# Reordering max and score tiles inside the stretches of a fused attention and MLP kernel

## The chip, the cores and the metric

The kernel runs on one core of a Trainium2 chip. A core has engines that run side by side, each with its own in-order queue: TensorE (PE, matmuls; its weight loads are listed apart as PEld), VectorE (DVE), ScalarE (ACT), GpSimd (POOL) and SyncE (SP, which issues the DMA transfers). They meet at semaphores. The metric is the device time of one execution in microseconds (us); lower is better.

## The reference

For x of shape 2048 x 640 the kernel computes a gated mix of two branches:

```
g = sigmoid(sum(x * gate_w))
q = x @ wq  (32 heads of 20);  k = x @ wk;  v = x @ wv   (one k and one v for all heads)
a = concat_heads(softmax(q k^T / sqrt(20)) v) @ wo
h = layernorm(x)                      # per token
u = gelu(h^T @ w1 + b1)               # 640 x 1728, over the token axis
b = (u @ w2 + b2)^T                   # back to 2048 x 640
out = g * a + (1 - g) * b
```

The gelu is the tanh form. Everything is float32; the products are made of a high and a low part of each operand (three matmuls: high by high, high by low, low by high).

## The kernel before

**Units.** Attention is cut into 32 units n (4 blocks of 512 queries by 8 groups of 4 heads), and each unit into 16 key blocks of 128. A *score tile* (written s, line 702) is one matmul of 62 rows by 512 columns into a PSUM bank; ACT turns it into probabilities with an exponential (line 711, tile p). The softmax needs each row's maximum first, and it is computed by *max tiles* (written m, line 490): the same product the other way round, reduced over the free axis by DVE (line 496, tile mp). A max tile of a later unit is made while an earlier unit's scores are. Per half of the array there are 1024 max tiles and 1024 score tiles. The probabilities of two key blocks times V are one "V group" (`pv_group`, line 737), 16 narrow matmul records in the trace, which the page's rows show as x16. Its sum is copied out by ACT (`part`, line 749, or `acc`, line 746) and added up by POOL (line 750). At the end of a unit DVE transposes, takes a reciprocal and transposes back (lines 763, 769, 777).

**Lanes and stretches.** s and m have at most 62 rows, and the MLP's matmuls (g) are cut to 64 rows, so two of them run at once in the two halves of the array. A *stretch* k is a list of g matmuls in one half (the side lane) with s and m matmuls in the other (the own lane); the halves swap in the next stretch. Then comes a V group, which takes the whole array. There are 84 stretches of the first MLP product (g at line 993, 24 g each; the first of them has no V group), 128 of the second (line 805, 20 or 21 g), 32 of the output projection of finished rows (line 938, 15 g), and after them a tail of 26 key blocks without max tiles. Ahead of them all stand the projections of x, the layer norm, the splitting of the weights, and a lead of 46 max tiles per half beside the first seven column blocks of the first product.

**What sets the order.** The order of each engine's queue is written out when the program is built; a small model of clocks (`clock`, `lanes`, `issue`; 0.232 us for an s or m, 0.147 for a g) merges the two lanes, and `bank_take` picks the PSUM bank of seven that the model frees first. The table `PATTERN` (line 1060) gives for each number of g matmuls the order of s and m in the own lane, and what the side lane has before and after its g matmuls (F). `main` trims or fills this list: the scores must be four tiles ahead of what the next V group eats, and the max tiles must be as many as `share` (line 1068) says. In the first product `share` compares the sum that the table plans with what is left; while it is over, it takes one m from the half that is more over, in stretches with k%4 = 1 alone. From the second product on it spreads what is left in proportion.

**The gelu chain.** A first-product tile ends every four stretches (k%4 = 3). `gelu` (line 534) has ACT add the bias (line 539) and puts the rest into `chain`: square (ACT, 543), the cube (`cube_p`, POOL, 560 and 561), `tanh` (ACT, 551), the product (`prod_p`, POOL, 564 and 565) and the split into high and low part (`high_p`, POOL, 582 and 583). `settle` takes one entry of the chain twice per stretch: once in the middle of the stretch's list, and once at its end, before the V group. The square comes at the end of its own stretch, the cube in the middle of the next, then an empty entry, and the tanh in the middle of the stretch with k%4 = 1.

Two halves that add into one bank must not overlap (`other_tile`, line 718): the first s or m after the last g waits for it on ACT or DVE, and the first g of the next stretch waits for that.

Of the kernel before, what the change touches and what calls it, by code (L numbers as in the profile page):

```python
# [40 lines left out]
def mix_kernel(ctx: ExitStack, tc: tile.TileContext, A_x, A_wq, A_wk, A_wv, A_wo,  # L41
# [5 lines left out]
    def f32(ap):  # L47
        return ap.bitcast(F32)
# [418 lines left out]
    def busy(engine, us):  # L467
        clock[engine] = max(clock[engine], clock["now"]) + us
# [63 lines left out]
    chain, ahead = [], []  # L532

    def gelu(d, fc, accs):
        both = fin.tile([P, D], F32, name="yo")
        xg, t1 = both[:, :HD2], both[:, HD2:]
        hi, lo = u_hi[d][:, fc, :], u_lo[d][:, fc, :]
        busy("act", 0.43)
        nc.scalar.activation(xg, accs[0][:, :HD2], AF.Identity, bias=bias[:, NS + fc:NS + fc + 1])

        def square():
            busy("act", 0.38)
            nc.scalar.activation(t1, xg, AF.Square)

        def add():
            nc.vector.tensor_add(xg, xg, accs[1][:, :HD2])  # L546
            square()

        def tanh():
            busy("act", 0.37)  # L550
            nc.scalar.activation(t1, t1, AF.Tanh, scale=GC * 0.044715)

        def high():
            nc.scalar.activation(hi, t1, AF.Copy)

        def low():
            nc.gpsimd.tensor_sub(lo, t1, f32(hi))

        def cube_p():
            nc.gpsimd.tensor_scalar(t1, t1, 1.0, 1.0 / 0.044715, op0=ALU.mult, op1=ALU.add)  # L560
            nc.gpsimd.tensor_mul(t1, t1, xg)

        def prod_p():
            nc.gpsimd.tensor_scalar(t1, t1, 1.0, 1.0, op0=ALU.mult, op1=ALU.add)
            nc.gpsimd.tensor_mul(t1, t1, xg)

        def plus(c):
            nc.scalar.activation(t1, t1, AF.Copy, bias=c)

        def mul():  # L570
            nc.gpsimd.tensor_mul(t1, t1, xg)

        def cubed():
            add()
            plus(1.0 / 0.044715)

        def tanh_plus():
            tanh()
            plus(1.0)

        def high_p():
            nc.gpsimd.tensor_copy(hi, t1)
            nc.gpsimd.tensor_sub(lo, t1, f32(hi))

        if len(accs) == 2:
            ends, ahead[:] = list(ahead), [high, low]
            if fc == PRO - 1:
                add()
                chain.extend((*ends, cube_p, None, tanh, prod_p, high_p))
            else:  # L590
                chain.extend((*ends, *[None] * (2 - len(ends)), cubed, None, None, mul, *[None] * 4, tanh_plus,
                              None, mul, None, None, None))
        else:
            chain.extend((square, cube_p, None, tanh, prod_p, high_p))

    def pop_chain():
        f = chain.pop(0) if chain else None
# [3 lines left out]
    with tc.tile_pool(name="psl", bufs=4, space=PSUM) as psl, \  # L601
# [9 lines left out]
        for fc in range(PRO):  # L611
            pu = [psb.tile([P, NB], F32, name=f"pu{r}") for r in range(2)]
            for hf in range(4):
                w1_upto(4 * fc + hf + 4)
                for f in [q_parts_due.pop(0) for _ in range(min(len(q_parts_due), 1 + fc // 5))] if fc else []:
                    f()
                wh, wl = w1t.pop(4 * fc + hf)
                for c in range(HS):
                    st = hf * HS + c
                    for k, (w, h) in enumerate(((wh, h_hi[0]), (wh, h_lo[0]), (wl, h_hi[0]))):  # L620
                        for r in range(2):
                            rows = slice(64 * r, 64 * r + 64)
                            nc.tensor.matmul(pu[r][:, :HD2], w[rows, c, :], h[rows, st, :],  # L623
                                             start=(st == 0 and k == 0), stop=(st == NS - 1 and k == 2))
                    done = [max(0, min(x, final) - skip) * LEAD // (final - skip) for x in (at, at + 1)]
                    if done[1] > done[0]:
                        lead()
                    at += 1
                    pop_chain()
                if fc == 1 and hf == 0:  # L630
                    new_q(0)
                if fc == PRO - 2 and hf == 2:
                    assert not q_parts_due
                    one_by_one[0] = False
                    fetch_max(0)
            gelu(0, fc, pu)
            if fc == PRO - 3:
                store_max(0)
# [340 lines left out]
    def b1_jobs(d, fc):  # L979
        hold = {}  # L980
        base = 4 * (d * FC + fc)

        def load():
            pass

        def mm(st, k, half):
            if not hold.get("n"):
                hold["p"], hold["n"] = ps_g.tile([P, NB], F32, name="g"), 0
            wh, wl = w1t[base + st // HS]
            w, h = ((wh, h_hi), (wh, h_lo), (wl, h_hi))[k]  # L990
            hold["n"] += 1
            r = slice(64 * half, 64 * half + 64)
            other_tile(half, nc.tensor.matmul(hold["p"][:, :HD2], w[r, st % HS, :], h[d][r, st, :],  # L993
                                              start=(hold["n"] == 1), stop=(hold["n"] == 6 * NS)))

        def done():
            gelu(d, fc, [hold["p"]])

        return load, [([[lambda h=h, st=st, k=k: mm(st, k, h) for h in range(2)]
                        for st in range(NS) for k in range(3)], done)]  # L1000
# [48 lines left out]
    def settle(wide=False):  # L1049
        for _ in range(2 if spare[0] else 1):  # L1050
            if later and (wide or spare[0] or not later[0][0]):
# [5 lines left out]
    sent, back_in = {0}, {0}  # L1057

    AHEAD, DRAIN, ENTER, FIRST = 4, 0.19, 0.138, 0.1
    PATTERN = {24: ("smssmsmmssmssmmm", "Fm"), 20: ("smsmssmmsmmssm", "mFs"), 21: ("smsmsmmssmmsmsm", "Fs"),  # L1060
               15: ("smsssmmmssms", "mFs"), 0: ("mmmmmmmmmmssss", "Fsmm")}

    def pattern(k):
        return PATTERN[len(ph[k][0]) if visits[k] else 0]

# [236 lines left out]
```

## Time and profile before

| what | value |
|---|---|
| median of 3 runs | 1632.41 us (1632.35 to 1633.01) |
| the profiled execution's own time | 1631.96 us |
| span of its trace | 1630.2 us |
| granted TensorE clock | 1.00 |
| busy: PE, DVE, ACT, POOL | 100%, 86%, 80%, 53% of the span |
| stages: lead and before, first product, second, projection, tail | to 170.7, to 665.7, to 1384.4, to 1546.5, to 1630.2 us |

The first stage of this table takes in the first two stretches of the first product. A row of the profile names the line, the engine, the operation, the output and inputs, the shapes and the count. The seven banks go from one use to the next, so a tile made by line 702 or 490 may carry the name ms, s or o of the bank; the line tells what it is. Rows of PE are modelled at their ends. A bracket at the end of a timeline row is the engine's idle time before it and what is taken to have ended it.

### The profile page before, as it was taken

The numbers are of one execution on the slowest core, as the hardware profiler recorded it, in microseconds if no ns is written. First come the engines' busy times: TensorE is split into PE (matmuls) and PEld (weight loads), VectorE is DVE, ScalarE is ACT, GpSimd is POOL, SyncE is SP. The second block draws the span as 40 slices with busy tenths as digits, with TensorE's granted clock in tenths as the row PEclk, the third lists the DMA queues.
The fourth block names the chain that finished last, engine by engine and source line by source line (L and its number), as shares of the span: only waits on it lengthen the run. The fifth ranks groups of instructions, "written<-read, shape, count | busy, mean of one in ns | idle before, by whom it ended". The sixth has DMA issues, their size and how long they took to land.

```text
span 1630.2 us, 39380 instructions
## 1 busy us (share of the span) xinstructions
PE 1622.6 (100%) x14877; PEld 1127.8 (69%) x14877; DVE 1400.5 (86%) x2404; ACT 1297.2 (80%) x2567; POOL 858.5 (53%) x974
## 2 busy tenths in 40 slices
PE   9999999999999999999999999999999999999998
PEld 7899766766676667666666666666666666666666
DVE  6689999999999999999999999899999999777723
ACT  4445778787887878888888888888888888999975
POOL 6568666767686767544544344354444432433400
PEclk9999999999999999999999999999999999999999
DMA  7655222322233223222212222222222112335421
GB/s 213 210 164 146 71 73 68 74 70 76 70 81 80 63 63 83 57 65 73 65 51 59 58 60 49 73 65 73 65 65 65 54 44 58 95 101 184 133 74 41
DMA packets 173603, 135.88 MB, mean 83 GB/s; under 512 B 32793, under 2 KB 139446, under 8 KB 173414
## 3 DMA queue, kind: packets, MB, share of 16 engines
q1 hardware_dynamic: 173126, 133.04, 29.6%
q8 instruction: 117, 1.92, 0.5%
q14 instruction: 72, 0.59, 0.1%
q10 hardware_dynamic: 288, 0.33, 0.1%
HBM read 100.27 MB, written 31.65 MB: 81 GB/s over the span
## 4 chain that ended last, share of the span: by engine, by line
PE 99%; ACT 0%; DVE 0%; issue 0%; DVEq 0%; ACTq 0%
PE ms L737 14%; PE g L805 11%; PE s L737 11%; PE s L702 9%; PE g L993 9%; PE ms L702 8%; PE ms L490 7%; PE s L490 7%; PE o L737 5%; PE pp L298 4%; PE pu L623 3%; PE o L702 3%; PE o L490 2%; PE g L938 2%; PE ml L490 1%; PE s L893 1%
## 5 line engine op out<-in xcount | busy, mean ns | idle before, releaser
L496 DVE TENSOR_REDUCE mp<-ms 128x1 f32<-128x512 f32 x859 | 566.1, 683 | 69.7 <-PE ms L490 61.9
L496 DVE TENSOR_REDUCE mp<-s 128x1 f32<-128x512 f32 x810 | 535.9, 682 | 44.1 <-PE s L490 37.9
L711 ACT ACTIVATE p<-s 128x512 f32<-128x512 f32 x906 | 534.2, 624 | 37.8 <-PE s L737 13.1
L711 ACT ACTIVATE p<-ms 128x512 f32<-128x512 f32 x847 | 498.3, 621 | 36.7 <-PE s L737 11.4
L750 POOL TENSOR_TENSOR acc<-acc,part 128x512 f32<-128x512 f32 x212 | 274.4, 1294 | 392.9 <-ACT part L749 373.9
L702 PE MATMUL s<-qst,kst 62*128 62x512 f32 x906 | 353.8, 413 | 0.0
L702 PE MATMUL ms<-qst,kst 62*128 62x512 f32 x847 | 335.5, 413 | 0.4 <-ACT p L711 0.4
L490 PE MATMUL ms<-kst,qmx 60*128 60x512 f32 x859 | 332.6, 410 | 0.3 <-ACT p L711 0.3
L490 PE MATMUL s<-kst,qmx 60*128 60x512 f32 x810 | 316.4, 409 | 0.6 <-DVE yo L546 0.5
L993 PE MATMUL g<-slot,wh 64*128 64x320 f32 x1344 | 306.8, 313 | 0.0
L993 PEld LDWEIGHTS g<-slot,wh 64*128 64x128 f32 x1344 | 221.5, 184 | 68.7 <-DVE mp L496 35.2
L129 POOL TENSOR_TENSOR wl<-wr,wh 128x512 fp32r<-128x512 f32 (+1 forms) x176 | 217.7, 1237 | 29.4 <-ACT wh L126 9.7
L737 PE MATMUL ms<-p,v_sb 128*32 128x512 f32 x1904 | 228.9, 598 | 0.0
L496 DVE TENSOR_REDUCE mp<-o 128x1 f32<-128x512 f32 x287 | 196.0, 683 | 20.5 <-PE o L490 18.3
L993 PE MATMUL g<-slot,wl 64*128 64x320 f32 x672 | 206.4, 307 | 0.0
L702 PEld LDWEIGHTS s<-qst,kst 62*128 62x128 f32 x906 | 166.7, 185 | 55.1 <-ACT p L711 31.7
L805 PE MATMUL g<-u,wh 64*128 64x320 f32 x864 | 196.7, 310 | 0.0
L805 PE MATMUL g<-slot,wh 64*128 64x320 f32 x864 | 196.3, 309 | 0.0
L702 PEld LDWEIGHTS ms<-qst,kst 62*128 62x128 f32 x847 | 156.2, 185 | 55.3 <-ACT p L711 43.0
L737 PE MATMUL s<-p,v_sb 128*32 128x512 f32 x1536 | 184.7, 598 | 0.0
L711 ACT ACTIVATE p<-o 128x512 f32<-128x512 f32 x280 | 174.1, 622 | 11.5 <-PE ms L737 5.5
L490 PEld LDWEIGHTS ms<-kst,qmx 60*128 60x128 f32 x859 | 157.5, 185 | 9.2 <-ACT p L711 3.3
(244 smaller groups left out, 3158.0 us busy)
## 6 DMA issues: line engine op xcount, KB each, us to landing
wr<-in_B_w_dram SPq DMA_DIRECT2D x136, 256.0 KB
qmx<-q_scr SPq DMA_DIRECT2D x192, 80.0 KB
qst<-q_scr SPq DMA_DIRECT2D x192, 80.0 KB
y_scr<-yo SPq DMA_DIRECT2D x16, 320.0 KB
slot<-o_scr SPq DMA_DIRECT2D x16, 320.0 KB
o_scr<-ot SPq DMA_DIRECT2D x124, 40.0 KB
o_scr<-acc SPq DMA_DIRECT2D x124, 40.0 KB
q_scr<-qh SPq DMA_DIRECT2D x19, 256.0 KB
```

The lines of the kernel that those rows point to most:

```text
L129: nc.gpsimd.tensor_sub(wl[:, :nv], wr[:, :nv], f32(wh[:, :nv]))
L298: nc.tensor.matmul(pp, w, t, start=first and n == 0, stop=not more and n == len(steps) - 1)
L490: nc.tensor.matmul(ms, qmax[n][64 * b:64 * b + 60, pr, qt * P:(qt + 1) * P], kst[64 * b:64 * b + 60, kq * NB:(kq + 1) * NB], start=True, s ...
L496: r = nc.vector.tensor_reduce(mtiles[n][:, c, kq:kq + 1], ms, axis=AX.X, op=ALU.max)
L623: nc.tensor.matmul(pu[r][:, :HD2], w[rows, c, :], h[rows, st, :], start=(st == 0 and k == 0), stop=(st == NS - 1 and k == 2))
L702: nc.tensor.matmul(s, kst[64 * b:64 * b + 62, kb * P:(kb + 1) * P], q[64 * b:64 * b + 62, pr, :], start=True, stop=True)
L711: e = nc.scalar.activation(p, s, AF.Exp, scale=SCALE)
L737: nc.tensor.matmul(o[32 * hh:32 * hh + 32, :], v_sb[:, kb + i, :], ptiles.pop((u, hh)), start=opened and i == 0, stop=(i == len(us) - 1) a ...
L750: nc.gpsimd.tensor_add(sums[0], sums[0], part)
L805: other_tile(half, nc.tensor.matmul(hold["p"][:, :HD2], w[r, i, :], u[d][r, fc, :], start=(hold["n"] == 1), stop=(hold["n"] == 6 * FC - 3)))
L938: other_tile(half, nc.tensor.matmul(hold["p"][:, :HD2], o[r, c, :], w[r, c, d * HD2:(d + 1) * HD2], start=(hold["n"] == 1), stop=(hold["n" ...
L993: other_tile(half, nc.tensor.matmul(hold["p"][:, :HD2], w[r, st % HS, :], h[d][r, st, :], start=(hold["n"] == 1), stop=(hold["n"] == 6 * NS)))
```

## The change

Three edits. In the table's entry for 24 g matmuls (first product) the own lane's order begins with an m, where it began with an s, and ends with two s, where it ended with three m; there are 8 of each as before. In the entry for 15 g (projection) the own lane has four m, where it had five, and its order alternates more. In the gelu chain one more empty entry stands ahead of the tanh, so that tanh comes at the end of the stretch with k%4 = 1, the product in the middle of the next and the split at that one's end; the last gelu of the lead keeps its chain.

```diff
@@ -591,7 +591,7 @@
         else:
-            chain.extend((square, cube_p, None, tanh, prod_p, high_p))
+            chain.extend((square, cube_p, None, None, tanh, prod_p, high_p))
@@ -1057,8 +1057,8 @@
     AHEAD, DRAIN, ENTER, FIRST = 4, 0.19, 0.138, 0.1
-    PATTERN = {24: ("smssmsmmssmssmmm", "Fm"), 20: ("smsmssmmsmmssm", "mFs"), 21: ("smsmsmmssmmsmsm", "Fs"),
-               15: ("smsssmmmssms", "mFs"), 0: ("mmmmmmmmmmssss", "Fsmm")}
+    PATTERN = {24: ("msmsmmssmsmmsmss", "Fm"), 20: ("smsmssmmsmmssm", "mFs"), 21: ("smsmsmmssmmsmsm", "Fs"),
+               15: ("smsmssmsmss", "mFs"), 0: ("mmmmmmmmmmssss", "Fsmm")}
```

## The prediction

> **What bounds the kernel now.** I read the page first: its engine lines and the chain that ended last.
>
> ```profile
> span 1630.2 us, 39380 instructions
> PE 1622.6 (100%) x14877; PEld 1127.8 (69%) x14877; DVE 1400.5 (86%) x2404; ACT 1297.2 (80%) x2567; POOL 858.5 (53%) x974
> PE 99%; ACT 0%; DVE 0%; issue 0%; DVEq 0%; ACTq 0%
> ```
>
> The chain is PE almost throughout, so the time is the sum of what PE's queue takes, and another engine counts only where it holds up a matmul. The windows view, cut where the stages begin, gives length, busy time (and instructions) of PE, PEld, DVE, ACT, POOL, then the granted clock, DMA share and GB/s:
>
> ```profile
> 170.71:665.68 494.97, 494.39 (x4661) 343.98 (x4657) 461.58 (x774) 396.43 (x801) 352.61 (x417) 1.00 0.28 72
> 665.68:1384.38 718.70, 718.35 (x6693) 480.65 (x6689) 652.99 (x1106) 612.10 (x1186) 317.62 (x348) 1.00 0.23 61
> 1384.38:1546.51 162.13, 162.13 (x1444) 103.14 (x1441) 124.67 (x211) 152.76 (x304) 66.57 (x72) 1.00 0.43 130
> ```
>
> These are the first product (82 stretches from the third on), the second product (128) and the projection (32, so 5.07 us each). DVE is 93% busy in the first; ACT is 94% busy in the third. Single stretches, cut from the first matmul after one probability-times-V group to the same point after the next:
>
> ```profile
> 292.20:298.20 6.00, 6.00 (x61) 4.20 (x57) 5.22 (x9) 4.51 (x9) 5.58 (x6) 1.00 0.54 135
> 298.20:304.26 6.06, 6.06 (x63) 4.19 (x59) 5.63 (x10) 5.40 (x11) 4.99 (x5) 1.00 0.10 27
> 406.51:412.45 5.94, 5.94 (x60) 4.18 (x57) 5.63 (x11) 4.86 (x10) 1.93 (x4) 1.00 0.39 103
> 237.13:243.62 6.49, 6.18 (x61) 4.17 (x58) 5.39 (x10) 4.98 (x10) 6.17 (x9) 1.00 0.28 74
> 285.72:292.20 6.48, 6.20 (x61) 4.17 (x57) 5.40 (x10) 4.97 (x10) 6.17 (x9) 1.00 0.30 66
> 460.52:466.76 6.24, 6.24 (x62) 4.15 (x58) 6.18 (x11) 4.62 (x9) 5.16 (x7) 1.00 0.01 1
> 622.88:629.16 6.28, 6.28 (x62) 4.36 (x58) 5.81 (x11) 4.86 (x10) 1.47 (x2) 1.00 0.37 90
> 647.27:653.67 6.40, 6.40 (x61) 4.31 (x57) 5.83 (x11) 4.86 (x10) 1.29 (x1) 1.00 0.01 1
> 671.73:677.97 6.24, 5.89 (x57) 3.77 (x53) 4.88 (x8) 5.08 (x10) 5.29 (x7) 1.00 0.49 144
> 677.97:683.53 5.56, 5.56 (x57) 3.71 (x54) 4.88 (x8) 4.65 (x9) 2.56 (x3) 1.00 0.10 29
> ```
>
> A full first-product stretch (24 g, 8 score, 9 max matmuls) takes 6.00 to 6.06, about 6.03. The third row lacks one max tile: 5.94. Rows four to eight are the stretches that stick out, the last two rows a long and a plain stretch of the second product. How a clean stretch ends, on PE's timeline (start, length):
>
> ```profile
> 301.59 0.40 PE L490 MATMUL ms<-kst,qmx 60*128 60x512 f32 x1
> 301.83 0.39 PE L490 MATMUL s<-kst,qmx 60*128 60x512 f32 x1
> 301.98 0.49 PE L490 MATMUL o<-kst,qmx 60*128 60x512 f32 x1
> 302.40 0.64 PE L737 MATMUL s<-p,v_sb 128*32 128x512 f32 x4
> ```
>
> The own lane's last tiles start 0.24 apart, the side lane's max tile follows the last g at 301.98, and the V group comes 0.42 after the last of them. Both lanes end within 0.15 us: the stretch has no room in either.
>
> **The counts.** Per half 1024 max tiles less 46 of the lead, 978, remain. The old table plans for the two halves 380 and 379 in the first product, 512 each in the second, 96 each in the projection: 988 and 987, so 10 and 9 too many. `share` drops one in each stretch with k%4 = 1 until none is over: 19 drops. The new projection pattern has one m less in its own lane, 16 per half: 972 and 971, that is 6 and 7 too few. Nothing is dropped then, and from the second product on `share` rounds the missing ones in: worked through its formula, 2 own lanes at the end of the second product and 11 in the projection get one extra. So the projection loses 32 - 11 = 21 max tiles, the first product gains 19 and the second 2.
>
> **The projection, 21 tiles out.** The end of such a stretch:
>
> ```profile
> 1437.53 0.39 PE L490 MATMUL s<-kst,qmx 60*128 60x512 f32 x1
> 1437.61 0.46 PE L702 MATMUL ms<-qst,kst 62*128 62x512 f32 x1
> 1437.87 0.49 PE L702 MATMUL s<-qst,kst 62*128 62x512 f32 x1
> 1438.29 0.64 PE L737 MATMUL ms<-p,v_sb 128*32 128x512 f32 x4
> ```
>
> 1437.53 is the own lane's eleventh tile, 1437.61 the side lane's score behind the 15 g, 1437.87 the own lane's twelfth; the V group follows 0.42 later. With eleven, the side lane's score is last, and by the same 0.42 the V group starts 0.26 earlier. Between 0.09 (what the missing tile is worth in the first product, 6.03 against 5.94) and 0.26, I take 0.24, since the row is of this very place: 21 x 0.24 = 5.0 saved. The Trainium skill, page "TensorE: Matmul & The Clock Gate", section "Back-to-back issue gap", puts a 512-column matmul at about 131 ns in a sustained stream; a saving of 21 x 0.131 = 2.8 would be the estimate by it. The rows above, 0.24 apart in one lane, do not agree with that figure.
>
> ACT is the cover to check, its timeline there:
>
> ```profile
> 1442.73 0.65 ACT L711 ACTIVATE p<-ms 128x512 f32<-128x512 f32 x1
> 1443.20 0.66 ACT L711 ACTIVATE p<-s 128x512 f32<-128x512 f32 x1
> 1443.68 0.59 ACT L952 ACTIVATE yo<-g,g_col 128x320 f32<-128x320 f32 x1
> 1444.57 0.69 ACT L711 ACTIVATE p<-s 128x512 f32<-128x512 f32 x1
> 1445.40 0.60 ACT L749 ACTIVATE part<-o 128x512 f32<-128x512 f32 x1
> ```
>
> Exponentials start 0.47 to 0.48 apart although each row reads 0.65. From the last one at 1444.57 ACT could take the copy from about 1445.05; it came at 1445.40. A stretch 0.24 shorter fits with 0.1 to spare, in the one of two that carries the L952 copy.
>
> **The first product, 19 tiles in.** 17 of the 19 stretches are clean now: 17 x (6.03 - 5.94) = 1.5 lost. The other two (6.49, 6.48) are long already, which is the next part. **The second product, 2 tiles in,** one own-lane tile each: 0.5 lost.
>
> **Tanh at stretch ends.** ACT's timeline in the 6.49 stretch, then PE's:
>
> ```profile
> 240.33 0.47 ACT L551 ACTIVATE yo<-yo 128x320 f32<-128x320 f32 x1 [0.45 <-POOL yo L561]
> 240.70 0.58 ACT L711 ACTIVATE p<-ms 128x512 f32<-128x512 f32 x1
> ```
>
> ```profile
> 240.54 0.49 PE L490 MATMUL o<-kst,qmx 60*128 60x512 f32 x1
> 241.34 0.50 PE L490 MATMUL ms<-kst,qmx 60*128 60x512 f32 x1 [0.30 <-ACT p L711]
> ```
>
> The tanh (L551) stood in mid-stretch, ACT idled 0.45 for POOL's cube, and the exponentials behind it came late; the last max tile found no free bank and started 0.80 after the one before, where 0.24 is usual. The stretch at 285.72 is its twin. Those at 622.88, 647.27 and 671.73 are of the same kind (k%4 = 1), the first two with all nine max tiles. After the change the tanh stands behind all exponentials of its stretch, ahead only of the V group's copy:
>
> ```profile
> 406.69 0.60 ACT L749 ACTIVATE part<-s 128x512 f32<-128x512 f32 x1 [1.53 <-issue]
> ```
>
> ACT idles 1.53 before that copy; the new order ends with scores about 0.8 later, so 0.7 is left for a tanh of 0.47. Behind it in POOL's queue the two products move half a stretch; POOL is 71% busy there and their reader, the second product, is a stage away. Gains against 6.03 (and 5.6 in the second product): 2 x 0.45 + 0.25 + 0.37 + 0.6 = 2.1. The bounds are 0 (the wait is another's) and 2.1; I take 2.1, since the tanh's own row carries the idle time.
>
> **The new order of 82 stretches.** The trace has no row of it. Scores and max tiles cost PE the same, so it costs only by banks. The spacings are 0.24 on PE, 0.48 on ACT and, by the DVE rows below, 0.60 on DVE (three reductions in 1.80), which begins 0.43 after a tile's start (237.47 on PE, 237.90 on DVE).
>
> ```profile
> 237.47 0.39 PE L490 MATMUL ms<-kst,qmx 60*128 60x512 f32 x1
> ```
>
> ```profile
> 237.90 0.69 DVE L496 TENSOR_REDUCE mp<-ms 128x1 f32<-128x512 f32 x1 [0.35 <-PE ms L490]
> ...
> 401.23 0.69 DVE L496 TENSOR_REDUCE mp<-ms 128x1 f32<-128x512 f32 x1 [0.49 <-PE ms L490]
> 404.33 1.88 DVE L496 TENSOR_REDUCE mp<-ms 128x1 f32<-128x512 f32 x3
> 406.13 0.68 DVE L496 TENSOR_REDUCE mp<-s 128x1 f32<-128x512 f32 x1
> ```
>
> In the new order the thirteenth tile starts at 2.9. By then seven max tiles have been issued and three reduced (0.43 + 3 x 0.60 = 2.2, the fourth at 2.8 with its bank given back just after), and six scores issued and three through ACT, which first copies the V group's sum: 4 + 3 = 7, all the banks there are. The same count for the old order reaches seven at its fifteenth tile, so neither order waits by it and neither has one to spare. Between waits of 0.2 per stretch (the 6.24 of 460.52) and a gain of 0.06 (6.06 to 6.00), I take zero, and 0.6 in all for the stretches after a unit's end, where DVE's transposes now meet nine reductions twice running.
>
> **Sum:** -5.0 + 1.5 + 0.5 - 2.1 + 0.6 = -4.5. The profiled execution took 1631.96 with 1.76 around its span, 0.45 under the median of 1632.41; from the median I predict 1627.9.
>
> **Rivals.** *One removed tile is worth 0.09, as in the first product*, because something other than the own lane ends the stretch (ACT at 94%, or the side lane). For it: the 5.94 row. Against it: the side lane's last tile at 1437.61. The projection then saves 21 x 0.09 = 1.9, the sum is -1.4: 1631.0. By the 131 ns of the Trainium skill's page named above the sum would be -2.3, an estimate of 1630.1; no row here shows a 512-column tile at that price.
>
> *Slower: DVE or the banks fall behind.* With nine reductions at 0.60, DVE needs 5.4 of 6.03, and the drops of k%4 = 1, which gave it rest, are gone. Where a max tile stands first, a late bank holds up both lanes, since PE takes its queue in order. If half of the 82 stretches wait 0.23 like the one at 460.52, that is 41 x 0.23 = +9.4, with -4.5 together +4.9: 1637.3. It decides from 20 such stretches on (20 x 0.23 = 4.6). For it: 93% busy. Against it: the 0.49 idle above, and the full stretches without a tanh, clean at 6.00 to 6.06.
>
> *Faster still:* ending on scores frees the banks sooner and every stretch runs like the 6.00 row or better: 82 x 0.04 = 3.3 more, 1624.6.
>
> **Chances.** The sum as it stands 0.47, the faster rival 0.13, the small saving 0.22, the slower rival 0.18. A change of 0.2% (3.3 us) is about what a measurement of this kernel can tell from none; 1629.1 is that limit below. Faster is therefore 0.60, same 0.22, slower 0.18. The likeliest case alone reaches from 1626 to 1629.5; the range takes in the small saving, most of the faster rival and the near part of the slower one: 1624.5 to 1635.0.
>
> **What would show it.** Projection stretches of 4.82 (21) beside 5.07 (11); max reductions by stage about 19 up, 2 up, 21 down; L551 with no stretch over 6.2 around it; k%4 = 1 stretches at 6.03. I am wrong if clean first-product stretches leave 6.00 to 6.06, if DVE is over 96% busy there, or if projection stretches stay at 4.95 or above.

## The result, and the profile after

The changed kernel took 1629.28 us (median of 16 runs, 1628.78 to 1629.83) against 1632.3 (16 runs, 1631.76 to 1633.32): a ratio of 0.9981, with a 95% interval of 0.9973 to 0.9989. That is 3.0 us faster; the forecast was 4.5 us (1627.9, range 1624.5 to 1635.0). The profiled span is 1627.5 after 1630.2, 2.7 less.

The page of the changed kernel, the lines that answer to those of before:

```profile
span 1627.5 us, 39247 instructions
PE 1617.5 (99%) x14877; PEld 1127.4 (69%) x14877; DVE 1386.5 (85%) x2404; ACT 1312.6 (81%) x2567; POOL 860.3 (53%) x974
PE 99%; ACT 1%; DVE 0%; issue 0%; DVEq 0%; ACTq 0%
```

It looks the same as before: PE carries the chain, and no engine's busy time moved by much over 1%. The stages tell more. The windows view of the changed kernel, columns as before, cut at the same stretches (first product from its third stretch, second product, projection):

```profile
171.37:663.69 492.32, 492.32 (x4679) 347.47 (x4676) 464.17 (x793) 411.97 (x801) 356.30 (x423) 1.00 0.28 73
663.69:1387.21 723.52, 720.27 (x6696) 479.95 (x6692) 648.44 (x1107) 613.54 (x1186) 317.74 (x347) 1.00 0.22 60
1387.21:1544.05 156.84, 156.84 (x1423) 99.93 (x1419) 111.84 (x188) 150.62 (x304) 64.52 (x68) 1.00 0.45 131
```

| stage | before | after | difference |
|---|---|---|---|
| up to the third stretch | 170.71 | 171.37 | +0.7 |
| first product, 82 stretches | 494.97 | 492.32 | -2.6 |
| second product, 128 stretches | 718.70 | 723.52 | +4.8 |
| projection, 32 stretches | 162.13 | 156.84 | -5.3 |

The tail after the projection takes 83.4 after 83.7. Two stages win and one loses clearly, and the one that loses is the stage whose table entries nobody touched. Single stretches of the changed kernel, cut as in the prediction:

```profile
297.48:303.44 5.96, 5.96 (x61) 4.22 (x57) 5.47 (x10) 5.50 (x11) 4.92 (x5) 1.00 0.10 22
237.42:243.38 5.96, 5.96 (x63) 4.22 (x59) 5.59 (x11) 5.08 (x10) 5.73 (x7) 1.00 0.22 57
219.26:225.48 6.22, 6.22 (x63) 4.30 (x59) 6.18 (x13) 4.74 (x9) 5.03 (x6) 1.00 0.15 39
267.20:273.66 6.46, 6.46 (x61) 4.27 (x57) 6.42 (x14) 4.95 (x9) 5.80 (x9) 1.00 0.18 42
703.29:709.14 5.85, 5.66 (x56) 3.73 (x52) 5.44 (x10) 5.24 (x10) 4.81 (x6) 1.00 0.43 117
1425.56:1430.35 4.79, 4.79 (x48) 3.06 (x44) 3.08 (x5) 4.74 (x10) 2.80 (x3) 1.00 0.44 138
1469.27:1474.35 5.08, 5.08 (x50) 3.22 (x47) 3.68 (x6) 4.90 (x10) 2.17 (x2) 1.00 0.83 239
```

- The plain full stretch of the first product takes 5.96, not 6.00 to 6.06. 70 of the 82 lie under 6.0; before, 22 did, most of them the ones with a dropped tile.
- The stretch that took 6.49 with the tanh in its middle (second row) is a plain one now.
- New long stretches stand at k%8 = 2, two stretches after the one that ends a unit of 16 key blocks: six of about 6.22 (third row), and four of 6.37 to 6.46 (fourth row).
- In the second product the plain 5.57 is kept, but once in eight stretches, 15 times from 703.29 on, stands one of 5.85 (fifth row). Three of the last five stretches of the stage are long as well: 6.08 and 6.06, where 5.66 and 5.64 stood (these two carry the two added max tiles), and the last one, 5.84 after 5.58.
- 21 of the 32 projection stretches have eleven own tiles and take 4.79 (sixth row), 11 have twelve; eight of these take 5.08, three 5.11 to 5.36.

Where the 0.07 us of a plain stretch went shows in the weight loads at its end, on PEld's timeline of the kernel before, and then of the changed kernel. In these traces a matmul's wait for a bank stands ahead of its weight load:

```profile
301.61 0.18 PEld L490 LDWEIGHTS s<-kst,qmx 60*128 60x128 f32 x1
301.98 0.18 PEld L490 LDWEIGHTS o<-kst,qmx 60*128 60x128 f32 x1 [0.18 <-ACT p L711]
```

```profile
301.06 0.18 PEld L702 LDWEIGHTS s<-qst,kst 62*128 62x128 f32 x1
301.15 0.18 PEld L490 LDWEIGHTS s<-kst,qmx 60*128 60x128 f32 x1
301.59 0.16 PEld L737 LDWEIGHTS ms<-p,v_sb 128*32 128x32 f32 x8 [0.25 <-ACT p L711]
```

Before, the side lane's last max tile waits 0.18 us for an exponential to give its bank back (on PE it starts 0.15 after the own lane's last tile; in the new order the last two tiles start 0.04 apart). Over the 82 stretches, idle time of 0.1 us or more stands ahead of the last tile's weight load 61 times before and 10 times after. The prediction had read the 0.15 between the two lanes' ends as a sign that neither lane had room. In the new order the last two loads are 0.09 apart with no idle time; the 0.25 ahead of the V group is what stands there in a plain stretch.

### The profile page after: what moved, and what is told of

Same layout as the page of the kernel before. It is cut to its first block, busy times and chain, and to the rows that moved or that the text cites. A ratio compares the mean times of both kernels' runs of the same rounds, so it can differ in the third digit from the quotient of the medians.

```text
span 1627.5 us, 39247 instructions
## 1 busy us (share of the span) xinstructions
PE 1617.5 (99%) x14877; PEld 1127.4 (69%) x14877; DVE 1386.5 (85%) x2404; ACT 1312.6 (81%) x2567; POOL 860.3 (53%) x974
## 4 chain that ended last, share of the span: by engine, by line
PE 99%; ACT 1%; DVE 0%; issue 0%; DVEq 0%; ACTq 0%
PE ms L737 15%; PE s L737 11%; PE g L805 11%; PE ms L702 10%; PE g L993 9%; PE s L702 8%; PE s L490 6%; PE ms L490 6%; PE pp L298 4%; PE pu L623 3%; PE o L702 3%; PE o L737 3%; PE o L490 2%; PE g L938 2%; PE ms L893 1%; PE ml L490 1%
## 5 line engine op out<-in xcount | busy, mean ns | idle before, releaser
L496 DVE TENSOR_REDUCE mp<-s 128x1 f32<-128x512 f32 x897 | 587.5, 679 | 84.7 <-PE s L490 64.7
L711 ACT ACTIVATE p<-ms 128x512 f32<-128x512 f32 x926 | 541.3, 614 | 45.5 <-PE ms L737 13.3
L496 DVE TENSOR_REDUCE mp<-ms 128x1 f32<-128x512 f32 x760 | 500.0, 678 | 46.6 <-PE ms L490 38.3
L711 ACT ACTIVATE p<-s 128x512 f32<-128x512 f32 x821 | 481.6, 613 | 34.6 <-PE ms L737 16.2
L702 PE MATMUL ms<-qst,kst 62*128 62x512 f32 x926 | 364.8, 412 | 0.1
L490 PE MATMUL s<-kst,qmx 60*128 60x512 f32 x897 | 356.1, 416 | 0.6 <-DVE yo L546 0.5
L702 PE MATMUL s<-qst,kst 62*128 62x512 f32 x821 | 326.1, 410 | 0.2 <-ACT p L711 0.2
L490 PE MATMUL ms<-kst,qmx 60*128 60x512 f32 x760 | 301.6, 411 | 0.0
L737 PE MATMUL ms<-p,v_sb 128*32 128x512 f32 x2144 | 257.8, 598 | 1.3 <-ACT p L711 1.3
L490 PEld LDWEIGHTS s<-kst,qmx 60*128 60x128 f32 x897 | 163.1, 185 | 7.9 <-ACT p L711 0.9
```

The lines of the kernel that those rows point to most:

```text
L490: nc.tensor.matmul(ms, qmax[n][64 * b:64 * b + 60, pr, qt * P:(qt + 1) * P], kst[64 * b:64 * b + 60, kq * NB:(kq + 1) * NB], start=True, s ...
L496: r = nc.vector.tensor_reduce(mtiles[n][:, c, kq:kq + 1], ms, axis=AX.X, op=ALU.max)
L702: nc.tensor.matmul(s, kst[64 * b:64 * b + 62, kb * P:(kb + 1) * P], q[64 * b:64 * b + 62, pr, :], start=True, stop=True)
L711: e = nc.scalar.activation(p, s, AF.Exp, scale=SCALE)
L737: nc.tensor.matmul(o[32 * hh:32 * hh + 32, :], v_sb[:, kb + i, :], ptiles.pop((u, hh)), start=opened and i == 0, stop=(i == len(us) - 1) a ...
```

## The experiments

### Each edit alone

The diff has three parts, so each was put into the kernel before by itself. The gelu edit:

```diff
-            chain.extend((square, cube_p, None, tanh, prod_p, high_p))
+            chain.extend((square, cube_p, None, None, tanh, prod_p, high_p))
```

> The kernel before with the gelu edit alone. Theory: in five stretches with k%4 = 1 the mid-stretch tanh held up the exponentials and through them a bank. With the tanh at the end the two at 6.49 and 6.48 us become 5.9, the two at 6.28 and 6.40 become about 6.05, the one of the second product falls from 6.24 to about 5.6; everything else stays: about 2.1 us saved, 1630.2. Rival: those stretches are long for another reason (POOL late, DVE's unit-end work), and less than 0.7 us is saved.

1629.40 us against 1632.14, ratio 0.9982 (0.9973 to 0.9991). The windows of this kernel: first product, second product, and the stretch that took 6.49:

```profile
170.65:663.39 492.74, 492.09 (x4660) 341.87 (x4657) 461.13 (x774) 397.62 (x801) 353.67 (x417) 1.00 0.28 72
663.39:1381.51 718.12, 718.12 (x6694) 480.64 (x6690) 652.71 (x1106) 612.28 (x1186) 317.72 (x348) 1.00 0.22 61
...
236.95:242.85 5.90, 5.88 (x61) 4.05 (x57) 5.37 (x10) 4.86 (x10) 5.67 (x7) 1.00 0.26 73
```

2.2 us come out of the first product and 0.6 out of the second, and none of the five stretches is long any more. The theory holds: the tanh in mid-stretch made these stretches long. The two of them that have all nine max tiles took 6.28 and 6.40 before and take 6.05 here; in the next kernel, which has the new order but keeps the tanh in mid-stretch, they take 6.21.

The order of the first product:

```diff
-    PATTERN = {24: ("smssmsmmssmssmmm", "Fm"), ...
+    PATTERN = {24: ("msmsmmssmsmmsmss", "Fm"), ...
```

> The kernel before with the new order of the first product alone (tanh in mid-stretch, projection as before, so the 19 drops stay). Theory (banks): in the old order the side lane's last max tile waits about 0.1 us for a bank in each full stretch, and the new order frees one in time. Full stretches go from 6.03 to 5.96 as in the changed kernel, the dropped ones stay at 5.9; the second product keeps its 718.7 us because the max tiles' count at its start is unchanged: 4 to 5 us saved in the first product, about 1627.8. Rival: the shorter full stretches of the changed kernel came from the tanh's move, and this one has 6.03 still: within 1 us of before.

1627.03 us, ratio 0.9968 (0.9955 to 0.998): by itself this edit gains more than the whole change. The windows of its three stages and two stretches, a full one and one with a dropped tile:

```profile
171.23:660.83 489.60, 489.60 (x4661) 345.17 (x4657) 454.45 (x773) 411.07 (x801) 352.61 (x417) 1.00 0.28 73
660.83:1379.39 718.56, 718.44 (x6694) 480.41 (x6691) 652.35 (x1106) 612.02 (x1186) 317.70 (x348) 1.00 0.22 61
1379.39:1541.59 162.20, 162.20 (x1445) 103.11 (x1441) 124.55 (x211) 152.75 (x304) 66.55 (x72) 1.00 0.43 130
296.56:302.51 5.95, 5.95 (x61) 4.22 (x57) 5.46 (x10) 5.49 (x11) 5.03 (x6) 1.00 0.07 18
260.82:266.77 5.95, 5.95 (x60) 4.11 (x56) 5.46 (x10) 5.08 (x10) 1.29 (x1) 1.00 0.00 0
```

5.4 us come out of the first product and nothing out of the others. A full stretch and a dropped one both take 5.95 here. The dropped one is still the one with the tanh in its middle, and its last tile waits (PEld's timeline of order_only):

```profile
264.49 0.18 PEld L490 LDWEIGHTS ms<-kst,qmx 60*128 60x128 f32 x1 [0.15 <-DVE mp L496]
```

So what the drop saves goes into that wait; the tanh's place is its likely cause, argued and not tried apart. What a drop is worth in the new order with the tanh at the end, lead56 below shows.

The projection pattern:

```diff
-               15: ("smsssmmmssms", "mFs"), ...
+               15: ("smsmssmsmss", "mFs"), ...
```

> The kernel before with the new projection pattern alone. Projection: 162.1 to about 156.8 us under every theory. Theory (phase): moving the 19 drops shifts where a unit's max tiles end against where a unit's scores end; the row-maximum reduction and the transposes meet in the same stretches of the second product, and its plain 5.57 becomes 5.85 once in eight stretches: 718.7 to about 723.5 with no other edit. Rival: that loss comes from the new order or the tanh, and the second product stays at 718 to 720. The first product gets its 19 tiles back in the old order with the tanh in mid-stretch: like the two full ones of before (6.28, 6.40), 17 stretches of 5.94 become 6.3, so 4 to 7 us more. In all 1632 to 1639 by the theory, about 1628 by the rival with free tiles.

1638.28 us, ratio 1.0036 (1.0023 to 1.0049): alone this edit is a loss. Its stages, one stretch of the first product that had dropped a tile before, and one of the second product:

```profile
171.32:673.03 501.71, 500.88 (x4679) 346.50 (x4676) 470.57 (x794) 396.42 (x801) 355.03 (x422) 1.00 0.28 72
673.03:1396.33 723.30, 720.18 (x6695) 479.82 (x6692) 648.56 (x1107) 613.20 (x1186) 317.92 (x347) 1.00 0.22 61
1396.33:1552.96 156.63, 156.63 (x1424) 99.80 (x1421) 111.78 (x188) 150.61 (x304) 64.47 (x68) 1.00 0.43 132
263.15:269.47 6.32, 6.32 (x61) 4.35 (x58) 5.79 (x11) 4.86 (x10) 1.30 (x1) 1.00 0.00 0
713.01:718.85 5.84, 5.65 (x56) 3.73 (x53) 5.47 (x10) 5.24 (x10) 4.81 (x6) 1.00 0.42 121
```

The projection gains its 5.5 us. The tiles it gives up cost 6.7 in the first product, where nine max tiles meet the mid-stretch tanh (6.32 where 5.94 stood), and 4.6 in the second product, with neither of the other two edits in the kernel. So the second product's loss comes with the moved tiles alone.

### Which end of the new order matters

```diff
-    PATTERN = {24: ("msmsmmssmsmmsmss", "Fm"), ...
+    PATTERN = {24: ("smmsmmssmsmmsmss", "Fm"), ...      # start_s
+    PATTERN = {24: ("msmsssmmssmssmmm", "Fm"), ...      # end_mmm
```

> The changed kernel with the first two tiles of the first product's order exchanged (s m m s m m s s m s m m s m s s): it begins with a score and ends with scores. Theory (DVE's early start frees banks): with a max tile first, DVE begins 0.34 us earlier in each stretch and one bank fewer is held when the side lane's last max tile comes; without it the count is eight of seven banks at that point, the tile waits 0.1 to 0.3 us, and a plain full stretch takes 6.05 to 6.25 where the changed kernel has 5.96: 7 to 20 us more in the first product. Rival (the end on scores is what shortens the stretch): 5.96 as in the changed kernel.

> The changed kernel with an order of the first product that begins with a max tile and ends with three (m s m s s s m m s s m s s m m m). Theory (DVE's early start): by the count of banks the side lane's last tile meets seven and waits under 0.1 us: plain stretches of 5.96 to 6.05. Rival (the end on scores is what shortens the stretch): 6.03 to 6.06, as in the kernel before. Only together with the exchange at the beginning do the two come apart clearly.

One run each: 1645.02 and 1644.72 us, beside 1632.15 for the kernel before on that chip. A window of a plain stretch and PEld's timeline at its end, first start_s:

```profile
301.70:307.88 6.18, 6.18 (x61) 4.30 (x57) 5.47 (x10) 5.47 (x11) 4.98 (x5) 1.00 0.12 31
```

```profile
305.27 0.18 PEld L702 LDWEIGHTS ms<-qst,kst 62*128 62x128 f32 x1
305.60 0.18 PEld L490 LDWEIGHTS ms<-kst,qmx 60*128 60x128 f32 x1 [0.15 <-DVE mp L496]
```

and end_mmm:

```profile
301.32:307.52 6.20, 6.20 (x62) 4.22 (x58) 5.56 (x10) 5.51 (x11) 4.99 (x5) 1.00 0.13 32
```

```profile
304.75 0.18 PEld L490 LDWEIGHTS ms<-kst,qmx 60*128 60x128 f32 x1
305.24 0.18 PEld L490 LDWEIGHTS o<-kst,qmx 60*128 60x128 f32 x1 [0.31 <-ACT p L711]
```

Exchanging the first two tiles costs 0.22 us in each stretch, as the count of banks said, and the last tile then waits for a max tile's bank. For end_mmm both theories were too low: 6.20, with a wait for an exponential's bank. The beginning and the end both matter, and the common thing is the bank of the last tile in the stretch: with seven banks in use, the exchange of two tiles in start_s shows in each of 82 stretches. The hand count was good for start_s (8 of 7) and missed end_mmm (7 of 7, "under 0.1").

### What the long stretches wait for

```diff
-            r = nc.vector.tensor_reduce(mtiles[n][:, c, kq:kq + 1], ms, axis=AX.X, op=ALU.max)
+            r = nc.vector.tensor_reduce(mtiles[n][:, c, kq:kq + 1], ms[:, :NB // 2], axis=AX.X, op=ALU.max)
```

> The changed kernel with each max tile reduced over 256 of its 512 columns, so that the maxima are of half the keys alone; this leaves out about half of DVE's main work. Theory: the long stretches after a unit's end (6.22 to 6.46 in the first product, 5.85 in the second) are DVE's backlog: all become plain (5.96 and 5.57), so the first product takes about 489 us and the second about 717.5. Rival (ACT, POOL or the transfer of the maxima): they stay.

1618.92 us in one run. Its second product, and the stretches that answer to 219.26, 267.20 and 703.29 above:

```profile
657.21:1377.82 720.61, 717.48 (x6696) 476.33 (x6693) 414.95 (x1106) 612.32 (x1186) 317.04 (x346) 1.00 0.22 61
...
216.78:222.71 5.93, 5.93 (x61) 4.13 (x57) 4.48 (x11) 4.89 (x10) 5.33 (x7) 1.00 0.21 63
264.86:271.21 6.35, 6.35 (x63) 4.31 (x59) 4.32 (x11) 4.84 (x9) 6.04 (x8) 1.00 0.33 80
696.37:702.22 5.85, 5.65 (x56) 3.73 (x53) 2.98 (x8) 5.24 (x10) 4.82 (x6) 1.00 0.22 59
```

The expectation split. The 6.22 stretches are DVE's backlog: with half the reduction work they are plain. The 6.46 ones fall only to 6.35, and the second product's 5.85 does not move at all although DVE is busy for 2.98 of it instead of 5.44. So that wait is not DVE's. The 2.9 us by which the stage is shorter here come from other stretches, most of all those at k%8 = 0, which the kernel before has too: 5.67 to 5.73 in the changed kernel, 5.58 here.

What stands in those stretches is seen on DVE's timeline, of the changed kernel ahead of 703.29 and then of the kernel before in the same place:

```profile
697.41 0.20 DVE L511 TENSOR_REDUCE mm<-mp 128x16 f32<-128x64 f32 x1
697.54 0.70 DVE L763 STREAM_TRANSPOSE ot<-acc 128x512 f32<-128x512 f32 x1
...
703.18 0.70 DVE L777 STREAM_TRANSPOSE acc<-ot 128x512 f32<-128x512 f32 x1
703.81 0.17 DVE L522 STREAM_TRANSPOSE mt<-mn 128x32 f32<-128x32 f32 x1
```

```profile
700.25 0.70 DVE L763 STREAM_TRANSPOSE ot<-acc 128x512 f32<-128x512 f32 x1
...
706.02 0.70 DVE L777 STREAM_TRANSPOSE acc<-ot 128x512 f32<-128x512 f32 x1
...
711.61 0.22 DVE L511 TENSOR_REDUCE mm<-mp 128x16 f32<-128x64 f32 x1
```

A unit's row maxima (L511, L522) are finished once per 32 max tiles of a half, a unit's output (L763, L777) once per 16 key blocks, and in the second product both come round every eight stretches. Before, 46 + 370 = 416 tiles of the first half and as many of the second were made when the second product began, which is 13 x 32, and the row maxima came two stretches after the first transpose. With the drops gone it is 426 and 425, and they come together with it.

The order of the queues is written by a model that charges DVE for all of these. So the next kernel takes the charge for the row-maximum work out of the model and leaves the work:

```diff
             mm = mmpool.tile([P, 16], F32, name="mm")
-            busy("dve", 0.14)
...
         mt = mpool.tile([P, 32], F32, name="mt")
-        busy("dve", 0.19)
```

> The changed kernel, in which the model that writes the order no longer charges DVE for the row-maximum work (0.14 us for the reduction, 0.19 for the transpose); the instructions themselves stay. With the reductions halved, the long stretches of 6.35 in the first product and 5.85 in the second were still there, so theory one: they are written into the order, the model sees DVE busy with this work and the transposes together and gives the last scores banks of exponentials that come back late. Without the charge about twelve of the 5.85 stretches become 5.57 and the second product takes 719 to 720; about 1625. Theory two: the work itself, 0.4 us on DVE beside the transposes, holds the banks: the second product stays at 723 us or over, 1629.

1625.69 us against 1632.19, ratio 0.9959 (0.9945 to 0.9973). Its second product, and the stretch that answers to 703.29:

```profile
663.51:1382.94 719.43, 718.95 (x6695) 479.68 (x6691) 648.86 (x1107) 612.35 (x1186) 318.13 (x347) 1.00 0.22 61
...
703.08:708.67 5.59, 5.59 (x56) 3.73 (x52) 5.48 (x11) 5.16 (x10) 4.55 (x6) 1.00 0.41 122
```

DVE does the same work in that stretch (5.48 us), in the same place (the reduction at 697.25 just ahead of the first transpose, the transpose of the maxima just behind the second one, here line 520 and line 775), and PE does not wait:

```profile
703.63 0.17 DVE L520 STREAM_TRANSPOSE mt<-mn 128x32 f32<-128x32 f32 x1
```

So 4.1 of the second product's 4.8 us were in the written order, not on DVE. PE's timelines show what the order does. In all fifteen 5.85 stretches the own and the side lane's last four tiles come as score, score, score, max; in the same fifteen places of the kernel before, of no_charge and of late_rowmax below they come as score, score, max, score. In the stretch from 703.29 they start 2.81, 3.15, 3.35 and 3.38 after its beginning and the V group at 4.00; in no_charge at 2.67, 2.90, 3.14 and 3.39, and the V group at 3.73. after_halfmax, with little work on DVE, has the changed kernel's order in these places and its length. One of the places where that order waits is seen on PEld's timeline of the changed kernel, 0.51 ahead of the V group where 0.25 is plain:

```profile
706.59 0.18 PEld L702 LDWEIGHTS ms<-qst,kst 62*128 62x128 f32 x1
707.29 0.16 PEld L737 LDWEIGHTS ms<-p,v_sb 128*32 128x32 f32 x8 [0.51 <-ACT p L711]
```

The next two kernels leave charge and work together and move both in time, in the changed kernel away from the transposes and in the kernel before onto them:

```diff
-        ms_done()
+        if not (k < 212 and k % 8 in (1, 2, 3)):       # late_rowmax, in the changed kernel
+            ms_done()
...
-        ms_done()
+        if not (84 <= k < 212 and k % 8 != 1):         # before_meet, in the kernel before
+            ms_done()
```

> The changed kernel, in which the reduction to a unit's row maxima is not issued at the end of stretches with k%8 = 1, 2 or 3 (up to the projection) but at the next one allowed. Nothing else is edited. Theory (phase): this takes 0.2 + 0.2 us of DVE work out of the stretches in which a unit's transposes stand. The fifteen or so 5.85 stretches of the second product go back to about 5.57 (4 us), and those of the first product at 6.37 to 6.46 to 6.2 (1 us): about 1624.5. Rival: the transposes and the full count of max tiles are enough for those waits, and under 1 us is gained.

> The kernel before, in which the row maxima of the second product are reduced only at the end of stretches with k%8 = 1, where the scale and transposes of a unit's end stand; nothing else is edited. Theory (phase): this brings the changed kernel's loss into the kernel before, 5.85 instead of 5.57 once in eight stretches: the second product goes from 718.7 to about 722.7, the first and the projection stay: about 1636. Rival (the loss needs the changed kernel's own stretches): 718.7 stays.

late_rowmax: 1624.66 us against 1632.14, ratio 0.9953 (0.994 to 0.9965), the fastest kernel here that leaves out no work. before_meet: 1634.66 in one run. The second product of each, late_rowmax first:

```profile
663.57:1383.00 719.43, 719.23 (x6695) 480.23 (x6692) 651.82 (x1107) 611.82 (x1186) 317.42 (x347) 1.00 0.22 61
```

```profile
665.35:1386.97 721.62, 718.16 (x6695) 479.60 (x6691) 648.09 (x1105) 613.81 (x1186) 319.57 (x349) 1.00 0.22 61
```

Moving the row maxima away gives back 4.1 of the 4.8 us, and moving them onto the transposes costs the kernel before 2.9 (4.0 were expected), with 15 stretches of 5.84 or 5.85. So it is the meeting in one place that brings the loss, and by no_charge it does so through the order that the model then writes. The first product gained only 0.7 in late_rowmax: the 6.22 stretches stay, as DVE's backlog should, and of the four of 6.37 to 6.46 three fell to 6.13 to 6.22. One stayed at 6.43. In that one the last two tiles come as max, score, as in the four of the changed kernel, and in the three that fell as score, max, as in a plain stretch; whether this order is the cause was not tried. In no_charge and in after_halfmax alike these four stay at 6.27 to 6.36, so for them either the work or the charge alone seems enough; this is argued and not shown.

### More max tiles in the lead

```diff
-LEAD = 46
+LEAD = 56
```

put on late_rowmax, with the row maxima kept out of k%8 under 4.

> The kernel with the late row maximum (now not issued at k%8 under 4), and 56 max tiles per half in the lead where there were 46. By the counts 20 tiles leave the stretches: 7 of the first product, 2 of the second, 11 of the projection. Theory: the projection loses 11 x 0.28 = 3.1 us, the second product 0.5, the first product 0.8 at three units' ends; the lead pays 10 pairs at 0.24 = 2.4. About 1622.6, 2 us under the kernel with the late row maximum alone. Rival: a pair in the lead costs more than 0.4 us, since it waits for its banks there, and nothing is gained.

1631.68 us, ratio 0.9996 (0.9987 to 1.0005): the rival was right. The stretches gained, against late_rowmax: the first product took 490.42 after 491.67, the projection 153.58 after 156.57; the second product took 719.86, 0.4 more. Seven first-product stretches drop a tile again; one of them and a full one, in windows:

```profile
247.86:253.72 5.86, 5.86 (x60) 4.13 (x56) 5.18 (x11) 5.08 (x10) 5.42 (x9) 1.00 0.05 9
307.15:313.10 5.95, 5.95 (x61) 4.22 (x57) 5.46 (x11) 5.49 (x11) 1.30 (x1) 1.00 0.24 70
```

A dropped tile is worth 0.09 in the new order, as it was in the old one. But the lead lost 10.4 us against late_rowmax, 1.04 for a pair. The windows from 96 us to the third stretch, of this kernel and then of the kernel before, say why:

```profile
96.00:182.26 86.26, 84.01 (x882) 72.32 (x880) 84.05 (x148) 40.05 (x79) 56.65 (x56) 1.00 0.48 127
```

```profile
96.00:170.71 74.71, 73.96 (x864) 68.28 (x862) 72.05 (x128) 39.80 (x79) 56.92 (x56) 1.00 0.54 149
```

DVE is busy for 72.05 of 74.71 us there already, so it had 2.7 us to spare, and the ten pairs ask 12.0 of it (72.05 to 84.05). With 56 the lead is DVE's stage: ahead of its max tiles' weight loads PE sat idle for 6.4 us in 16 waits for DVE, where it had been 0.7 in 3. So a pair costs nearly two reductions (2 x 0.60). PE's rows fill both windows as well, but twenty more tiles at 0.24 would be under 5 us.

## Why the prediction was right, and where not

The time fell inside the range and the sign was right, but that the sum came so near is luck: two misses in good part cancelled. The new order gained 5.4 us and stood in the sum as zero; the units' ends and the second product lost some 8 us and stood in it as 1.1. Of the signs that the prediction named, the 21 projection stretches of about 4.82 came. The clean first-product stretches left 6.00 to 6.06, which it had named as a sign of being wrong.

- **The projection, 21 tiles out.** Predicted 5.0, measured 5.3. The count of 21 short stretches was exact; each saved 0.28, a little over the 0.26 read from the timeline. The copy on ACT did not lengthen the short stretches. Three of those with twelve tiles take 5.11 to 5.36, 0.4 in all; whether ACT is their cause was not tried. The 131 ns per 512-column matmul of the Trainium skill (page "TensorE: Matmul & The Clock Gate", section "Back-to-back issue gap") would have given 2.8; no run here bears that out for two lanes of 60 to 64 rows.
- **Tanh at stretch ends.** Predicted 2.1, measured 2.8 alone (2.2 in the first product, 0.6 in the second). Reading the idle time ahead of the tanh's row was right.
- **19 tiles into the first product.** Predicted a loss of 0.09 for each of 17, 1.5 in all. lead56 shows the same 0.09 for the new order (5.95 against 5.86), so the term stands; what the tiles cost beyond it is at the units' ends, below.
- **The new order, taken as zero.** This is the largest term that was mis-sized: 5.4 us gained in the first product (order_only). The step that failed is "neither order waits by it". The count found the old order at seven of seven banks and stopped there; PEld's row at 301.98, with 0.18 us of idle time for an exponential, was to be had, and the 0.15 between the lanes' ends was that wait. The rival "faster still" (3.3 us more) had named this gain, for the end on scores alone; start_s shows that the beginning on a max tile is needed as well.
- **Units' ends in the first product, 0.6.** The ten stretches at k%8 = 2 run 0.26 to 0.50 over the plain 5.96, 3.5 us in all; one of them was long before as well (6.24). The mechanism was the named one, DVE with nine reductions twice running (after_halfmax makes six of them plain), and the size was off by a factor of more than five. It is the slower rival in small: 10 stretches, where 20 would have decided.
- **The second product.** Two more tiles were predicted at 0.5; the stage lost 4.8. The two tiles themselves cost 0.42 each (6.08 and 6.06 at the stage's end). Nothing in the prediction asked what the moved tiles do to the place of the row maxima, or to the order that the model writes from it. 15 stretches at 0.28 over plain are 4.2 of the loss. The count that would have told it, 416 = 13 x 32 against 426, used only numbers of the prediction's own paragraph on counts.

Summed as measured, the edits alone give -2.7 (tanh), -5.1 (order) and +6.1 (projection) in median time, -1.7 together, and the whole change -3.0. So they help one another by 1.3. A likely part of it is that the returned tiles meet a mid-stretch tanh in proj_only and none in the whole change; the edits were not run in pairs, so this is not shown.

## What to carry to other kernels

Where two engines empty a small ring of PSUM banks, look at the idle time ahead of the weight loads of the last tiles before each barrier: a wait of 0.18 us there did not show on the matmul's row or in PE's busy share, and taking it away made each of the plain stretches 0.07 us shorter. When work is moved between stages, work out where the periodic side jobs (here a unit's row maxima and a unit's output) land afterwards. A queue order written from a model can wait for what the model feared: here a charge for work that would have fitted cost 4.1 us.

## What the runs showed that was not expected

The kernel before left DVE only 2.7 of 74.71 us to spare in its lead, though the page's shares put PE at 100% and DVE at 86% over the whole span. And the biggest loss of the change stayed when DVE's work in its stretch was cut from 5.44 to 2.98 us, and went away when the work was left at 5.48 and the order written otherwise.
